# Second layer of a fused kernel: low parts of its weights on VectorE, conversion issued by steps, other banks and four buffers for its output blocks

## The chip, the cores and the metric

The kernel runs on one core of one Trainium2 chip. The time is that of the device for one run, in microseconds (us); shorter is better. A run is compared by the median of its executions. One further execution is profiled, and every row below comes from that one.

## What is computed

A gated linear attention over 4 batches of 8 heads, 768 positions and 48 features, then two feed-forward layers on 3072 tokens of 384 features, the first gated with 1536, the second with 2048 hidden features. All of it is in float32.

```python
def _attn_ref(q, k, v, f_logit):
    f = 1.0 / (1.0 + np.exp(-f_logit))
    for t in range(S):
        state = f[:, :, t, :, None] * state + np.einsum('bhd,bhe->bhde', k[:, :, t], v[:, :, t])
        y[:, :, t] = np.einsum('bhd,bhde->bhe', q[:, :, t], state)

def _moe_ref(x, w_gate, w_val, w_out):
    gate = 1.0 / (1.0 + np.exp(-(x @ w_gate)))
    return (gate * (x @ w_val)) @ w_out

def _moe2_ref(x, w_in, w_out):
    h = x @ w_in
    return (h * (1.0 / (1.0 + np.exp(-1.702 * h)))) @ w_out
```

## The kernel before, in words

**Products of two parts.** Each float32 product is made of three matmuls of a narrower type: every operand is a high part and a low part (the number less its high part), and `mm3` adds high x high, high x low and low x high in PSUM (lines 369 to 371, and 470 to 472 in the second layer's output). ScalarE makes the high parts, VectorE the low ones (`split`, lines 381 and 382). For each chunk of 128 hidden features of the second layer (`m2_in`), ScalarE applies the sigmoid (line 455), VectorE multiplies (line 456), then ScalarE and VectorE split the product into `gh` and `gl`. In the first layer `m1_gate` and `m1_val` do the same with two projections (lines 395 and 401).

**Weights.** They lie in memory as 64-bit numbers, in units of 3 x 384 columns; units 0 to 11 are the first layer's, 12 to 22 the second's. A unit is loaded by SyncE into a buffer `wd` (`w_load`; in the second layer there are two such buffers), turned into 32-bit numbers on VectorE by three instructions through one scratch tile `wt` (`w_conv`, lines 337, 341 and 344), and split (`w_split`): ScalarE writes the high part (line 351), and the low part is made by VectorE for units 0 to 11 and by GpSimd for units 12 to 22 (line 353). The split tile takes the place of a first-layer unit that TensorE has done with. Later every unit is loaded again for a check of its range (`w_check`, on ScalarE).

**Tiles and stages.** The first layer goes over the tokens in 8 tiles of 256 to 512, and attention runs beside it, some way ahead. The second layer goes over 6 tiles of 512 tokens in 16 chunks each; a chunk is a projection (9 matmuls of 512 columns) and, two chunks later, 12 matmuls of 384 columns into four output blocks (`m2_out`). The units 12 to 22 are converted while the last tile of the first layer runs, and a little beyond.

**PSUM.** Three banks in a ring hold projections (`ps_g`, tag `gv`). Three hold the first layer's output (`ps_x`, tags `x20`, `x21`, `x22`), which is copied out by ScalarE, VectorE and ScalarE in this order (lines 426 and 428); two are attention's (`ps_a`, tag `at`). In the second layer blocks 0 to 2 of a tile use `ps_x` and block 3 `ps_a`. Copies of the finished blocks (lines 476 and 478) go to three buffers `o`, and from there to memory by SyncE.

**Order.** Every step is put down with a position in a plan by `at(pos, ...)`, the steps are sorted by position and each engine gets its instructions in that order. `group(n)` is what the plan counts for 9 matmuls of n columns, `P8` the position of the last tile of the first layer, `P2` that of the second layer, `PACE2` the distance of two of the units 12 to 22. Steps of these units are held in that order on VectorE and ScalarE (`held_back`).

Of the kernel before, what the change touches and what calls it, by code (L numbers as in the profile page):

```python
# [48 lines left out]
PACE2 = 6.9  # L49
# [6 lines left out]
def fused_kernel(ctx, tc, qk, lf, vu, vn, wts, consts, out):  # L56
# [277 lines left out]
    def w_conv(u):  # L334

        lw, hw = st["wd", u][:, :, 0], st["wd", u][:, :, 1]
        nc.vector.tensor_scalar(
            out=wt, in0=hw, scalar1=3, scalar2=0x3FFFFFF8,
            op0=ALU.logical_shift_left, op1=ALU.bitwise_and,
        )  # L340
        nc.vector.scalar_tensor_tensor(  # L341
            out=wt, in0=hw, scalar=-0x40000000, in1=wt, op0=ALU.bitwise_and, op1=ALU.bitwise_or
        )
        nc.vector.scalar_tensor_tensor(  # L344
            out=lw, in0=lw, scalar=29, in1=wt, op0=ALU.logical_shift_right, op1=ALU.bitwise_or
        )

    def w_split(u):
        s = st.pop(("wd", u)).bitcast(F32)[:, :, 0]
        w = wp.tile([128, 2, WU], F32R, tag="w", name="w")  # L350
        nc.scalar.activation(out=w[:, 0], in_=s, func=AF.Copy)
        eng = nc.vector if u < NF1 else nc.gpsimd
        eng.tensor_tensor(out=w[:, 1], in0=s, in1=w[:, 0].bitcast(F32), op=ALU.subtract)  # L353
        for m in range(3):
            st["w", 3 * u + m] = w[:, :, DM * m:DM * m + DM]
# [103 lines left out]
    def m2_out(j, fc):  # L459
        gh, gl = st.pop(("g", L2 + j, fc))  # L460
        w = st["w", W2 + 2 * fc + 1]
        if fc == 0:
            st["ops"] = [
                (ps_x if k < 3 else ps_a).tile([128, DM], F32, tag=f"x2{k}" if k < 3 else "at", name="ops")
                for k in range(TT // 128)
            ]
        for m in range(TT // 128):
# [5 lines left out]
            if fc == NF2 - 1:  # L473
                o = st["late"].tile([128, DM], F32, tag="o", bufs=3, name="o")
                if m % 2 == 1:
                    nc.vector.tensor_copy(out=o, in_=ps)
                else:
                    nc.scalar.activation(out=o, in_=ps, func=AF.Copy)
                r0 = j * TT + m * 128
                nc.sync.dma_start(out=out[r0:r0 + 128, :], in_=o)  # L480
# [24 lines left out]
    def count():  # L505
        low, one = st["low"]
        cnt = ps_a.tile([1, 1], F32, tag="at", name="cnt")
# [140 lines left out]
    for u in range(NF1):  # L648
        p = need[u]
        at(p - 13, w_load, u)  # L650
        at(p - 7, w_conv, u)
        at(p - 5, w_split, u)
    for u in range(NF1, NU):
        p = P8 + 8 + (u - NF1) * PACE2
        at(p - 4, w_load, u)
        at(p, w_conv, u)
        at(p + 2, w_split, u)
# [6 lines left out]
    def held_back(pos, fn, args):  # L664
# [3 lines left out]
        if fn in (w_conv, w_split) and args[0] >= NF1:  # L668
# [297 lines left out]
```

## Time and profile before

| what | value |
| --- | --- |
| median of 3 runs | 1012.57 us (1011.74 to 1015.92) |
| the profiled execution, its own time | 1011.5 us |
| its span | 1009.7 us |
| mean granted clock of TensorE | 0.976 |
| TensorE busy | 966.4 us (96%) |
| VectorE busy | 621.8 us (62%) |
| ScalarE busy | 393.2 us (39%) |
| GpSimd busy | 150.1 us (15%) |

The span runs from the first to the last instruction; what is between it and the run's time lies outside of the trace. In rows, PE is TensorE, DVE VectorE, ACT ScalarE, POOL GpSimd and SP SyncE. Matmuls overlap one another, and the ends of them are modelled, so their pace is read from start to start. The clock is a share of full speed.

### The profile page before, as it was taken

What the parts mean: (1) busy time and instruction counts of PE and PEld (TensorE: products, weight loads), DVE (VectorE), ACT (ScalarE), POOL (GpSimd) and SP (SyncE); (2) the same over time, 40 slices, a digit from 0 to 9 for tenths busy, and PEclk for the clock granted to TensorE, in tenths of its full rate; (3) what the DMA queues carried; (4) which work ended last, traced back from release to release, by engine and by line L of the source; (5) the groups of instructions that cost most, each with busy time, mean ns of one, the idle gap of its engine ahead of it and who ended that gap; (6) DMA issues with size and microseconds to landing.
All of it is one profiled execution on the core that took longest, in us unless ns stands there. A gap on an engine that the chain in (4) does not pass through costs nothing.

```text
span 1009.7 us, 17235 instructions
## 1 busy us (share of the span) xinstructions
PE 966.4 (96%) x6978; PEld 857.7 (85%) x6978; DVE 621.8 (62%) x1073; ACT 393.2 (39%) x744; POOL 150.1 (15%) x157
## 2 busy tenths in 40 slices
PE   6689899999999999999999889999999999999997
PEld 4579899899999888888888668989999989999996
DVE  7799978876778767777658786343433433433332
ACT  3335333333343422232332326888632322322322
POOL 2311212312132312222104331000000000000000
PEclk8589999999999999999999999999999999999999
DMA  5664312221231321121033347787210000000001
GB/s 151 231 208 186 103 39 86 83 62 54 63 91 54 92 60 46 46 77 54 7 156 141 141 172 291 276 300 265 102 63 1 24 10 1 32 1 1 32 1 35
DMA packets 29736, 96.86 MB, mean 96 GB/s; under 512 B 4496, under 2 KB 16912, under 8 KB 23760
## 3 DMA queue, kind: packets, MB, share of 16 engines
q1 hardware_dynamic: 29504, 95.57, 28.3%
q8 instruction: 57, 0.93, 0.4%
q14 instruction: 31, 0.25, 0.1%
q10 hardware_dynamic: 144, 0.10, 0.0%
HBM read 84.25 MB, written 9.44 MB: 93 GB/s over the span
## 4 chain that ended last, share of the span: by engine, by line
PE 70%; DVE 13%; ACT 6%; DMA 5%; issue 5%; POOL 1%; SPq 0%; ACTq 0%; DVEq 0%; POOLq 0%
PE gv L369 13%; PE gv L371 12%; PE gv L370 12%; PE ops L470 6%; PE ops L472 6%; PE ops L471 5%; DMA wd<-in_wts 4%; PE x2ps L369 3%; PE x2ps L371 3%; PE x2ps L370 3%; PE yt L282 2%; PE sc L197 2%; DVE wt L341 2%; DVE wd L344 2%; DVE gl L382 1%
## 5 line engine op out<-in xcount | busy, mean ns | idle before, releaser
L369 PE MATMUL gv<-xh,w 128*128 128x512 f32 (+2 forms) x864 | 313.5, 363 | 7.6 <-DVE g L401 3.8
L371 PE MATMUL gv<-xh,w 128*128 128x512 f32 (+2 forms) x864 | 308.1, 358 | 1.0 <-DVE w L353 0.9
L370 PE MATMUL gv<-xl,w 128*128 128x512 f32 (+2 forms) x864 | 308.4, 357 | 0.6 <-DVE xl L314 0.4
L382 DVE TENSOR_TENSOR gl<-g,gh 128x512 fp32r<-128x512 f32 (+2 forms) x192 | 138.5, 723 | 117.8 <-ACT gh L381 91.5
L381 ACT ACTIVATE gh<-g 128x512 fp32r<-128x512 f32 (+2 forms) x192 | 110.5, 577 | 237.7 <-DVE g L401 173.0
L369 PEld LDWEIGHTS gv<-xh,w 128*128 128x128 f32 x864 | 164.3, 190 | 30.2 <-DVE g L401 4.6
L371 PEld LDWEIGHTS gv<-xh,w 128*128 128x128 f32 x864 | 163.4, 190 | 22.2 <-DVE w L353 1.6
L370 PEld LDWEIGHTS gv<-xl,w 128*128 128x128 f32 x864 | 164.4, 190 | 18.1 <-DVE xl L314 1.3
L456 DVE TENSOR_TENSOR g<-g,gv 128x512 f32<-128x512 f32 x96 | 66.0, 688 | 161.4 <-ACT g L455 161.4
L470 PE MATMUL ops<-w,gh 128*128 128x384 f32 x384 | 129.9, 338 | 1.3 <-ACT x L428 1.2
L472 PE MATMUL ops<-w,gl 128*128 128x384 f32 x384 | 129.6, 338 | 0.0
L471 PE MATMUL ops<-w,gh 128*128 128x384 f32 x384 | 129.0, 336 | 0.0
L455 ACT ACTIVATE g<-gv 128x512 f32<-128x512 f32 x96 | 57.0, 594 | 140.9 <-PE gv L371 140.9
L370 PE MATMUL x2ps<-gl,w 128*128 128x256 f32 (+2 forms) x288 | 97.6, 340 | 3.8 <-DVE gl L382 3.8
L369 PE MATMUL x2ps<-gh,w 128*128 128x256 f32 (+2 forms) x288 | 96.2, 339 | 1.4 <-ACT gh L381 1.4
L371 PE MATMUL x2ps<-gh,w 128*128 128x256 f32 (+2 forms) x288 | 96.8, 337 | 0.0
L395 ACT ACTIVATE g<-gv 128x256 f32<-128x256 f32 (+2 forms) x96 | 47.0, 489 | 122.4 <-PE gv L371 121.8
L232 DVE STREAM_TRANSPOSE kn<-kh 32x128 f32<-32x128 f32 x288 | 87.1, 302 | 4.2
L401 DVE TENSOR_TENSOR g<-g,gv 128x256 f32<-128x256 f32 (+2 forms) x96 | 52.6, 548 | 56.9 <-PE gv L371 55.1
L470 PEld LDWEIGHTS ops<-w,gh 128*128 128x128 f32 x384 | 72.1, 188 | 7.1 <-ACT x L428 1.6
L471 PEld LDWEIGHTS ops<-w,gh 128*128 128x128 f32 x384 | 72.1, 188 | 4.0
L472 PEld LDWEIGHTS ops<-w,gl 128*128 128x128 f32 x384 | 72.0, 188 | 0.3 <-DVE gl L382 0.3
(99 smaller groups left out, 1087.2 us busy)
## 6 DMA issues: line engine op xcount, KB each, us to landing
wd<-in_wts SPq DMA_DIRECT2D x46, 1152.0 KB, 5.2
QKF<-in_qk SPq DMA_DIRECT2D x42, 192.0 KB, 3.4
QKF<-in_lf SPq DMA_DIRECT2D x22, 256.0 KB, 2.9
vnt<-in_vn SPq DMA_DIRECT2D x24, 192.0 KB, 3.1
U<-in_vu SPq DMA_DIRECT2D x48, 96.0 KB, 2.7
x<-x2d SPq DMA_DIRECT2D x6, 768.0 KB, 5.6
out_y<-o SPq DMA_DIRECT2D x24, 192.0 KB, 1.9
x2d<-x SPq DMA_DIRECT2D x4, 768.0 KB, 3.8
```

The source lines that it names most:

```text
L232: nc.vector.transpose(out=kn[32 * b:32 * b + 32, :, 32 * a:32 * a + 32], in_=kh[32 * a:32 * a + 32, :, 32 * b:32 * b + 32],)
L369: nc.tensor.matmul(out=ps, lhsT=wh, rhs=xh, start=first, stop=False)
L370: nc.tensor.matmul(out=ps, lhsT=wh, rhs=xl, start=False, stop=False)
L371: nc.tensor.matmul(out=ps, lhsT=wl, rhs=xh, start=False, stop=last)
L381: nc.scalar.activation(out=gh, in_=g, func=AF.Copy)
L382: (eng or nc.vector).tensor_tensor(out=gl, in0=g, in1=gh.bitcast(F32), op=ALU.subtract)
L401: nc.vector.tensor_tensor(out=g, in0=g, in1=pv, op=ALU.mult)
L455: nc.scalar.activation(out=g, in_=ph, func=AF.Sigmoid, scale=1.702)
L456: nc.vector.tensor_tensor(out=g, in0=g, in1=ph, op=ALU.mult)
L470: nc.tensor.matmul(out=ps, lhsT=gh[:, ts], rhs=w[:, 0], start=fc == 0, stop=False)
L471: nc.tensor.matmul(out=ps, lhsT=gh[:, ts], rhs=w[:, 1], start=False, stop=False)
L472: nc.tensor.matmul(out=ps, lhsT=gl[:, ts], rhs=w[:, 0], start=False, stop=fc == NF2 - 1)
```

## The change

The low parts of units 12 to 22 move from GpSimd to VectorE. The three conversion instructions and the two of the split become steps of their own, at five positions instead of two, and the distance of two units grows from 6.9 to 7.4 of the plan. The blocks 0 and 1 of an output tile go to the two banks of `ps_a`, blocks 2 and 3 take turns through the three of `ps_x`; the one-value tile `cnt` moves to the ring of projections. There are four output buffers instead of three, and the copy of the very last block is made in two halves, by VectorE and ScalarE.

```diff
-PACE2 = 6.9
+PACE2 = 7.4
...
-    def w_conv(u):
+    def w_conv(u, step):
...
-    def w_split(u):
+    def w_high(u):
+        s = st["wd", u].bitcast(F32)[:, :, 0]
+        w = st["wu", u] = wp.tile([128, 2, WU], F32R, tag="w", name="w")
+        nc.scalar.activation(out=w[:, 0], in_=s, func=AF.Copy)
+
+    def w_low(u):
         s = st.pop(("wd", u)).bitcast(F32)[:, :, 0]
-        w = wp.tile([128, 2, WU], F32R, tag="w", name="w")
-        nc.scalar.activation(out=w[:, 0], in_=s, func=AF.Copy)
-        eng = nc.vector if u < NF1 else nc.gpsimd
-        eng.tensor_tensor(out=w[:, 1], in0=s, in1=w[:, 0].bitcast(F32), op=ALU.subtract)
+        w = st.pop(("wu", u))
+        nc.vector.tensor_tensor(out=w[:, 1], in0=s, in1=w[:, 0].bitcast(F32), op=ALU.subtract)
...
             st["ops"] = [
-                (ps_x if k < 3 else ps_a).tile([128, DM], F32, tag=f"x2{k}" if k < 3 else "at", name="ops")
-                for k in range(TT // 128)
+                (ps_a if m < 2 else ps_x).tile(
+                    [128, DM], F32, tag="at" if m < 2 else f"x2{(2 * j + m) % 3}", name="ops"
+                )
+                for m in range(TT // 128)
             ]
...
-                o = st["late"].tile([128, DM], F32, tag="o", bufs=3, name="o")
-                if m % 2 == 1:
+                o = st["late"].tile([128, DM], F32, tag="o", bufs=4, name="o")
+                if j == N2 - 1 and m == 3:
+                    nc.vector.tensor_copy(out=o[:, 0:192], in_=ps[:, 0:192])
+                    nc.scalar.activation(out=o[:, 192:], in_=ps[:, 192:], func=AF.Copy)
+                elif m % 2 == 1:
...
-        cnt = ps_a.tile([1, 1], F32, tag="at", name="cnt")
+        cnt = ps_g.tile([1, 1], F32, tag="gv", name="cnt")
...
     for u in range(NF1, NU):
         p = P8 + 8 + (u - NF1) * PACE2
         at(p - 4, w_load, u)
-        at(p, w_conv, u)
-        at(p + 2, w_split, u)
+        for step in range(3):
+            at(p + (0, 0.9, 2.4)[step], w_conv, u, step)
+        at(p + 3.8, w_high, u)
+        at(p + 5.2, w_low, u)
...
-        if fn in (w_conv, w_split) and args[0] >= NF1:
+        if fn in (w_conv, w_high, w_low) and args[0] >= NF1:
```

Nothing before unit 12 moves on any engine. The order of VectorE before, in the last tile of the first layer, from the product (`g`) of one chunk to the low half (`gl`) of the second after it (`wt` and `wd` are a unit's conversion):

```order
L401 TENSOR_TENSOR g<-g,gv 128x512
L382 TENSOR_TENSOR gl<-g,gh 128x512
L337 TENSOR_SCALAR wt<-wd 128x1152
L341 SCALAR_TENSOR_TENSOR wt<-wd,wt 128x1152
L344 SCALAR_TENSOR_TENSOR wd<-wd,wt 128x1152
L401 TENSOR_TENSOR g<-g,gv 128x512
L382 TENSOR_TENSOR gl<-g,gh 128x512
L337 TENSOR_SCALAR wt<-wd 128x1152
L341 SCALAR_TENSOR_TENSOR wt<-wd,wt 128x1152
L344 SCALAR_TENSOR_TENSOR wd<-wd,wt 128x1152
L401 TENSOR_TENSOR g<-g,gv 128x512
L382 TENSOR_TENSOR gl<-g,gh 128x512
```

The order of VectorE now, at the same place, three products with what stands between and behind them (`w` is a low part):

```order
L407 TENSOR_TENSOR g<-g,gv 128x512
L388 TENSOR_TENSOR gl<-g,gh 128x512
L347 SCALAR_TENSOR_TENSOR wd<-wd,wt 128x1152
L359 TENSOR_TENSOR w<-wd,w 128x1152
L407 TENSOR_TENSOR g<-g,gv 128x512
L388 TENSOR_TENSOR gl<-g,gh 128x512
L338 TENSOR_SCALAR wt<-wd 128x1152
L343 SCALAR_TENSOR_TENSOR wt<-wd,wt 128x1152
L347 SCALAR_TENSOR_TENSOR wd<-wd,wt 128x1152
L407 TENSOR_TENSOR g<-g,gv 128x512
L359 TENSOR_TENSOR w<-wd,w 128x1152
L388 TENSOR_TENSOR gl<-g,gh 128x512
```

Before, each product had a whole conversion behind it; now a conversion can lie on both sides of a product, and its low part follows on VectorE.

The order of VectorE now at the seam of the layers, from the copy of the first layer's middle block (`x`) on, two products of the second layer and what stands around them (`xl` are low parts of the second layer's next input):

```order
L432 COPY x_6425<-x2ps 128x512
L388 TENSOR_TENSOR gl<-g,gh 128x512
L338 TENSOR_SCALAR wt<-wd 128x1152
L343 SCALAR_TENSOR_TENSOR wt<-wd,wt 128x1152
L462 TENSOR_TENSOR g<-g,gv 128x512
L347 SCALAR_TENSOR_TENSOR wd<-wd,wt 128x1152
L388 TENSOR_TENSOR gl<-g,gh 128x512
L452 TENSOR_TENSOR xl<-x_6452,xh 128x512 x2
L359 TENSOR_TENSOR w<-wd,w 128x1152
L462 TENSOR_TENSOR g<-g,gv 128x512
L452 TENSOR_TENSOR xl<-x_6452,xh 128x512
L338 TENSOR_SCALAR wt<-wd 128x1152
```

Before, the same stretch had no low parts `w`, and its last unit came with the first of these chunks; now a unit more is converted here.

The last copies with their waits, ScalarE now (the names with numbers are buffers and blocks of the last tile; `o_9440` is the last):

```order
L489 ACTIVATE o_9422<-ops_9014 128x384 [waits DMAHW1_49,PE_49]
L489 ACTIVATE o_9434<-ops_9016 128x384 [waits DMAHW3_49,PE_49]
L485 ACTIVATE o_9440<-ops_9017 128x192 [waits DMAHW4_49,DMAHW0_49,DVE_49]
```

and VectorE now:

```order
L487 COPY o_9428<-ops_9015 128x384 [waits DMAHW2_49,PE_49]
L484 COPY o_9440<-ops_9017 128x192 [waits DMAHW4_49,PE_49]
```

VectorE's half waits for TensorE and for a buffer, ScalarE's half waits for VectorE. Before, VectorE copied the whole block.

## Rows read from the trace of the kernel before

**Rows 1.** Windows: stretch, then us, PE, PEld, DVE, ACT, POOL busy, PEclk, DMA.

```profile
565.00:570.00 5.00, 3.02 (x14) 2.19 (x13) 4.16 (x5) 0.85 (x2) 0.04 (x1) 1.00 0.64 236
595.00:600.00 5.00, 1.78 (x6) 1.25 (x7) 4.04 (x3) 1.38 (x3) 2.67 (x1) 0.96 0.18 31
600.00:605.00 5.00, 4.44 (x14) 3.19 (x12) 3.38 (x4) 2.17 (x4) 0.32 (x1) 0.70 0.87 362
```

**Rows 2.** Waits of PE, 540 to 660 us: total, times, longest.

```profile
PE gv L369 <- DVE g L401: 3.8, 2, 2.0
PE x2ps L370 <- DVE gl L382: 2.6, 2, 2.3
```

**Rows 3.** Windows, of the whole loss and of a stretch without waits.

```profile
558.29:608.18 49.89, 41.13 (x168) 31.50 (x166) 40.06 (x35) 17.48 (x26) 16.21 (x6) 0.97 0.43 161
575.67:587.91 12.24, 12.24 (x55) 10.13 (x54) 9.51 (x9) 4.18 (x6) 3.30 (x2) 1.00 0.45 177
```

**Rows 4.** Groups by line, DVE, 540 to 600 us: busy us, mean ns, idle before.

```profile
L341 DVE SCALAR_TENSOR_TENSOR wt<-wd,wt 128x1152 int32<-128x1152 int32 x8 | 15.7, 1958 | 0.3
L382 DVE TENSOR_TENSOR gl<-g,gh 128x512 fp32r<-128x512 f32 x8 | 12.5, 1566 | 7.2 <-ACT gh L381 7.2
L337 DVE TENSOR_SCALAR wt<-wd 128x1152 int32<-128x1152 int32 x8 | 9.8, 1224 | 2.8 <-DMA wd<-in_wts 2.8
...
L401 DVE TENSOR_TENSOR g<-g,gv 128x512 f32<-128x512 f32 x8 | 5.5, 682 | 0.9 <-ACT g L395 0.9
```

**Rows 5.** Groups by line, POOL, 540 to 600 us.

```profile
L353 POOL TENSOR_TENSOR w<-wd,w 128x1152 fp32r<-128x1152 f32 x7 | 19.6, 2794 | 38.6 <-ACT w L351 33.4 <-DMA wd<-in_wts 5.2
```

**Rows 6.** Timeline, DVE: start us, us, instruction, idle before.

```profile
569.81 0.69 DVE L382 TENSOR_TENSOR gl<-g,gh 128x512 fp32r<-128x512 f32 x1 [0.70 <-ACT gh L381]
...
595.92 2.75 DVE L382 TENSOR_TENSOR gl<-g,gh 128x512 fp32r<-128x512 f32 x1 [1.22 <-ACT gh L381]
```

**Rows 7.** Instructions on tile wd: min/median/max ns, first and last start us.

```profile
L337 DVE TENSOR_SCALAR wt<-wd x23: 742/751/3271, 36.5 to 607.8; 128x1152 int32<-128x1152 int32 x23
L341 DVE SCALAR_TENSOR_TENSOR wt<-wd,wt x23: 1343/1359/3760, 37.4 to 608.6; 128x1152 int32<-128x1152 int32 x23
L344 DVE SCALAR_TENSOR_TENSOR wd<-wd,wt x23: 1341/1359/3748, 39.2 to 610.5; 128x1152 int32<-128x1152 int32 x23
L351 ACT ACTIVATE w<-wd x23: 1228/1257/1301, 41.9 to 611.9; 128x1152 fp32r<-128x1152 f32 x23
...
L353 DVE TENSOR_TENSOR w<-wd,w x12: 1331/1356/1683, 43.2 to 130.1; 128x1152 fp32r<-128x1152 f32 x12
```

**Rows 8.** Timeline, POOL, the low part beside the second row of rows 6.

```profile
595.45 2.67 POOL L353 TENSOR_TENSOR w<-wd,w 128x1152 fp32r<-128x1152 f32 x1 [5.42 <-ACT w L351]
```

**Rows 9.** DMA issues of the page: KB each, median us to landing.

```profile
wd<-in_wts SPq DMA_DIRECT2D x46, 1152.0 KB, 5.2
```

**Rows 10.** Timeline, PE, the last projection's matmul and the first output block's.

```profile
604.05 0.39 PE L371 MATMUL gv<-xh,w 128*128 128x512 f32 x1
605.63 0.44 PE L470 MATMUL ops<-w,gh 128*128 128x384 f32 x1 [1.19 <-ACT x L428]
```

**Rows 11.** Windows, a stretch of the second layer.

```profile
750.00:800.00 50.00, 50.00 (x253) 45.28 (x252) 18.29 (x27) 15.97 (x28) 0.00 (x0) 1.00 0.00 1
```

**Rows 12.** Timeline of the end: the last matmul and the last copy.

```profile
1002.77 0.34 PE L472 MATMUL ops<-w,gl 128*128 128x384 f32 x1
1004.11 0.56 DVE L476 COPY o<-ops 128x384 f32<-128x384 f32 x1 [1.45 <-DMA out_y<-o]
```

**Rows 13.** Groups by line and shape, DVE, a copy of 256 columns.

```profile
L426 DVE COPY x<-x2ps 128x256 f32<-128x256 f32 x1 | 0.4, 409 | 0.0
```

**Rows 14.** Groups by line and shape, ACT, copies out of PSUM.

```profile
L298 ACT ACTIVATE xr<-yt 32x128 f32<-32x128 f32 x24 | 6.5, 269 | 0.3
...
L478 ACT ACTIVATE o<-ops 128x384 f32<-128x384 f32 x12 | 5.8, 479 | 3.2 <-PE ops L472 3.2
L428 ACT ACTIVATE x<-x2ps 128x512 f32<-128x512 f32 x8 | 4.7, 593 | 5.4 <-PE x2ps L371 5.4
```

More of the change, by code (lines that the diff above doesn't have):

```diff
@@ L332, in w_load @@
         st["wd", u] = d
-    def w_conv(u):
+    def w_conv(u, step):
         lw, hw = st["wd", u][:, :, 0], st["wd", u][:, :, 1]
[L337 to L346, printed above, removed]
-    def w_split(u):
+        if step == 0:
+            nc.vector.tensor_scalar(
+                out=wt, in0=hw, scalar1=3, scalar2=0x3FFFFFF8,
+                op0=ALU.logical_shift_left, op1=ALU.bitwise_and,
+            )
+        elif step == 1:
+            nc.vector.scalar_tensor_tensor(
+                out=wt, in0=hw, scalar=-0x40000000, in1=wt, op0=ALU.bitwise_and, op1=ALU.bitwise_or
+            )
+        else:
+            nc.vector.scalar_tensor_tensor(
+                out=lw, in0=lw, scalar=29, in1=wt, op0=ALU.logical_shift_right, op1=ALU.bitwise_or
+            )
+    def w_high(u):
[3 more added lines that the diff above has]
+    def w_low(u):
         s = st.pop(("wd", u)).bitcast(F32)[:, :, 0]
-        w = wp.tile([128, 2, WU], F32R, tag="w", name="w")
-        nc.scalar.activation(out=w[:, 0], in_=s, func=AF.Copy)
-        eng = nc.vector if u < NF1 else nc.gpsimd
-        eng.tensor_tensor(out=w[:, 1], in0=s, in1=w[:, 0].bitcast(F32), op=ALU.subtract)
+        w = st.pop(("wu", u))
+        nc.vector.tensor_tensor(out=w[:, 1], in0=s, in1=w[:, 0].bitcast(F32), op=ALU.subtract)
         for m in range(3):
@@ L463, in m2_out @@
             st["ops"] = [
-                (ps_x if k < 3 else ps_a).tile([128, DM], F32, tag=f"x2{k}" if k < 3 else "at", name="ops")
-                for k in range(TT // 128)
+                (ps_a if m < 2 else ps_x).tile(
+                    [128, DM], F32, tag="at" if m < 2 else f"x2{(2 * j + m) % 3}", name="ops"
+                )
+                for m in range(TT // 128)
             ]
@@ L650, in fused_kernel @@
         at(p - 13, w_load, u)
-        at(p - 7, w_conv, u)
-        at(p - 5, w_split, u)
+        for step in range(3):
+            at(p - 7, w_conv, u, step)
+        at(p - 5, w_high, u)
+        at(p - 5, w_low, u)
     for u in range(NF1, NU):
@@ L655, in fused_kernel @@
         at(p - 4, w_load, u)
-        at(p, w_conv, u)
-        at(p + 2, w_split, u)
+        for step in range(3):
+            at(p + (0, 0.9, 2.4)[step], w_conv, u, step)
+        at(p + 3.8, w_high, u)
+        at(p + 5.2, w_low, u)
     for u in range(NU):
```

## The prediction

> **What bounds the kernel now.** TensorE is busy 96% of the span, so time can only be won where it stands still. I read the views from coarse to fine: the busy table of the page, then 5-us windows over the seam between the two layers, then the waits of TensorE, then single rows. In [rows 1] the reader sees three windows in which TensorE works 3.02, 1.78 and 4.44 of 5 us, the last two at a granted clock of 0.96 and 0.70. [rows 2] names what it waited for there: VectorE's products `g` (3.8 us in two waits) and VectorE's low halves `gl` (2.6 us).
>
> The whole loss of this seam can be counted. Between 575.67 and 587.91 nothing waits: 54 matmuls of 512 columns in 12.24 us, 0.2267 us each [rows 3]. Between 558.29 and 608.18 the order holds 154 of these and 12 of 384 columns (168 with the ones at the edges). A step of the second layer, 9 of the one and 12 of the other, takes 4.15 us (253 matmuls in 50.00 us, 21 to a step, [rows 11]), which leaves 0.176 us for one of 384 columns. So 154 x 0.2267 + 12 x 0.176 = 37.0 us of work stand in 49.9 us: **12.9 us lost**. This is more than the named waits, since it holds short restarts and the fallen clock: the means of 0.96 and 0.70 [rows 1] make 0.4 and 3.0 us at 1.2 instead of 2.4 GHz, half of which, 1.7 us, is lost.
>
> Why VectorE is late there: it converts the second layer's weights, in units of 1152 columns. In [rows 4] its three long forms average 1958, 1566 and 1224 ns between 540 and 600 us, while the same instructions undisturbed take 1359 [rows 7], 690 [rows 6] and 751 ns [rows 7]. Eight of each: 8 x (0.60 + 0.88 + 0.47) = 15.6 us of stretch. GpSimd made 7 low parts in that time [rows 5], so each of them costs VectorE 2.2 us. One pair shows how: GpSimd's low part begins at 595.45 and ends at 598.12 [rows 8]; VectorE's `gl` begins at 595.92, takes 2.75 us instead of 0.69 and ends 0.55 us after GpSimd does [rows 6].
>
> In the old order most of these steps carry one whole unit between two products. That is 0.75 + 1.36 + 1.36 [rows 7], plus 2.2 of stretch, plus `gl` 0.69 and the product 0.68 [rows 4, 6]: 7.0 us, against 27 matmuls x 0.2267 = 6.12 us for TensorE. VectorE is the bound of this seam and falls back 0.9 us a step until TensorE waits.
>
> **The change part by part.**
>
> *Low parts on VectorE.* GpSimd's 11 instructions leave, 11 of 1.36 us come to VectorE (12 of that form ran on VectorE in the first layer, [rows 7]). They take the stretch of 2.2 us a unit with them, since GpSimd then has nothing left to do. VectorE's work for a unit goes from 3.47 + 2.2 = 5.7 to 3.47 + 1.36 = 4.83 us.
>
> *Pace and steps.* Units come every 7.4 instead of 6.9 of the plan's microseconds. The plan counts 0.4245 ns a column, 27 x 512 x 0.4245 ns = 5.87 us a step, and the trace shows 6.12, so a unit comes every 1.26 steps, 7.7 us. VectorE then needs 4.83 + 1.26 x (0.68 + 0.69) = 6.6 us of every 7.7, or 85%. The fullest steps of the new order (low part, `gl` and three conversion rows between two products) need 1.36 + 0.69 + 3.47 + 0.68 = 6.2 us against 6.12, and no more than two of them follow each other; the others need 4.1 to 4.8. None falls back as now. So the waits on `g`, `gl` and `gh` go, and the clock has no reason to fall. I take all of the 12.9 us as the gain, and look for what is late next.
>
> *What waits behind the new instructions.* A low part on VectorE waits for ScalarE's high part (1.26 us, [rows 7]) and holds the next product behind it. In most places `gl` or a product stands between, so 1.26 - 0.69 = 0.6 us of VectorE's time stays idle per unit: 85% becomes 93%. On SyncE a load of raw weights waits for the low part that frees its buffer. From a unit's first step to its low part's end it takes some 6.8 us, the load 5.2 us to land [rows 9] and 0.4 to issue, and the buffer's next turn comes after two units, 15.4 us: 3 us are left. The other loads on that queue (tiles of the second layer's input) are wanted tens of microseconds later. Cost nothing, covered by this gap. Units end about 5 us later by the plan; the last is wanted in the 15th step of the second layer, some 40 us after it is ready.
>
> *Output blocks.* Blocks 0 and 1 go to banks that attention has long left, so the old wait of 1.19 us for the first copy out of layer one [rows 10] has no place. Block 2 now takes the bank that the *last* copy empties, on ScalarE behind a `gh`. Its first matmul starts 16 slots after layer one's last one starts (10 x 0.2267 + 6 x 0.176 = 3.3 us). That last matmul ends 0.39 after its start and a copy takes 0.59 [rows 14], so the copy could end at 1.0 if the product before `gh` is on time, which leaves 2.3 us. One conversion row of 1.36 us ahead of the product fits, two don't. Bounds: 0 and 1.35 us (what that place loses today: 1.19 idle, and the 0.16 by which a matmul's modelled end, at 0.39, stands behind its slot, [rows 10]). In the five steps there (4.15 us each) VectorE's rows, split parts and the copy of `x` taken at 0.69 like `gl`, need 4.1, 4.2, 5.4, 4.2 and 4.1 us, 22.0 against 20.8: nearly full but with two steps of lag to spend. I take 0.5 us, nearer to zero, since the fallback is spread over the lag.
>
> The one-value count moved to the ring of three banks for projections takes a turn there once, whose next user comes three projections later. Nothing.
>
> *End.* The last output copy waits for a buffer: TensorE is done at 1002.77 + 0.34 = 1003.11, the copy begins at 1004.11 and takes 0.56 [rows 12], so it ends at 1004.67. With four buffers it can start at about 1003.15. Of the halves, VectorE's 192 columns lie below the 409 ns of 256 [rows 13]; the slope to 0.56 for 384 [rows 12] gives 0.34. ScalarE's lie between 269 ns for 128 and 479 for 384 [rows 14]: 0.32. Side by side they end at 1003.5, a gain of 1.2 us. But the new order shows a wait on VectorE at ScalarE's half: one after the other they end at about 1003.85. I take **0.8 us**, and keep 1.2 as the other end. At the ends of the other tiles the fourth buffer gives TensorE nothing, since it waits for no output copy there.
>
> No run here shows two engines reading one bank together. The Trainium skill, PSUM — Partial Sum Buffer, "PSUM bank collisions raise a hardware error", says that two engines on the same bank and quadrant at once are an error, reads against reads included; by it halves of one block must go one after the other, which is what the order shows, and the gain is 0.8.
>
> Sum against the profiled execution, 1011.5 us (span 1009.7): 12.9 - 0.5 + 0.8 = 13.2 us, so **998.3**. The median of the runs, 1012.57, stands 1.1 above that execution; I put about two thirds of it on the forecast: **999.0 us**.
>
> **The rivals.**
>
> *VectorE is full at the seam (20%).* For: 22.0 us of rows in 20.8 us, waits on ScalarE not counted. Against: before that stretch it has 7 to 15% to spare. Price: block 2 waits 1.35 us instead of 0.5, the 1.2 us of fallback become waits, and a clock that falls once costs 1.7 us as it does now. That is 3.8 more: about 1003.
>
> *The stretch is VectorE's own (7%).* If GpSimd didn't cause it, a unit costs 5.7 + 1.36, with products 8.8 us every 7.7. Over ten units 11 us are lost instead of 12.9; with the end's 0.8 this gives about 1009, no change. Against: the undisturbed rows of the same forms, and that the long ones end just after GpSimd's.
>
> The Trainium skill, Perfetto Trace Analysis, "Optimizing Scalar/DVE Operations", advises work off VectorE, even to GPSIMD, when VectorE is saturated, and adds that the two share a read port, so that it might not help. Taken by its first half the move is wrong and this rival or the next follows; the trace agrees with the second half, 2.2 us of stretch against 1.36 us of work.
>
> *Slower: VectorE stands before the low part (5%).* Same stretch, and each low part waits out ScalarE's high part of 1.26 us with the product queued behind: 10.1 us a unit every 7.7, 23 us lost over ten units instead of 12.9, about 1021. It decides from 9.0 us a unit on (7.7 + 1.3, where today's loss is reached); without the stretch even a full wait of 1.26 gives 7.9.
>
> That the change doesn't do what it says is left out: the order has GpSimd's 11 rows gone and VectorE's 11 there, and the last half's wait is counted.
>
> **How the numbers follow.** Forecast 68%, rivals 20, 7 and 5%. The range reaches from 996.5 (no wait at block 2, halves side by side, all of the median's offset left out) to 1005 (the first rival with the median's offset and a microsecond of waits in the first steps of the second layer). About 0.5% (5 us) is what a measurement of this kernel can tell from no change. Faster by more than that: the forecast and the first rival, 88%; within it 7%; slower 5%.
>
> **What would show it.** Right: between 558 and 608 us TensorE is busy in every window at a clock of 1.00; VectorE's long forms average 1.36, 0.69 and 0.75 us; GpSimd has no row after attention's last; the first output block waits for nothing; the last copy starts 0.05 us behind the last matmul and ScalarE's half behind VectorE's. Wrong: forms that stay stretched without GpSimd; a wait of `ops` on a copy of `x` of over 1.4 us; idle time of VectorE before its low parts of more than a microsecond each; a projection that waits for weights.

## The result, and the profile after

The changed kernel takes 997.5 us (median of four runs, 996.43 to 1000.45), the kernel before 1012.15 in the same comparison. The ratio is 0.9854 with a 95% interval of 0.982 to 0.9888: faster by 1.1 to 1.8%. One of the four executions of experiment 6 below took 1883.38 us; why is not known, and its median is that of the other three.

The profiled execution of the changed kernel took 1000.45 us, the longest of its four, with a span of 998.7. It need not be compared by its end: the first 450 us of the kernel vary by up to 4 us from run to run, while from 500 us on two executions of the changed kernel agree within hundredths (experiment 11). So I use a yardstick that every trace here has: from ScalarE's gate sigmoid in the first layer near 500 us (the 83rd of its kind) to the last one of the kernel (the 192nd). The timeline of ScalarE, before and after, each row with its start, its length and the idle time ahead of it:

```profile
500.34 0.60 ACT L395 ACTIVATE g<-gv 128x512 f32<-128x512 f32 x1 [2.72 <-PE gv L371]
...
996.94 0.60 ACT L455 ACTIVATE g<-gv 128x512 f32<-128x512 f32 x1 [2.20 <-PE gv L371]
```

```profile
503.00 0.60 ACT L401 ACTIVATE g<-gv 128x512 f32<-128x512 f32 x1 [2.71 <-PE gv L377]
...
985.74 0.60 ACT L461 ACTIVATE g<-gv 128x512 f32<-128x512 f32 x1 [2.20 <-PE gv L377]
```

It is 496.60 us before and 482.74 after: **13.86 us** gone. The seam alone, by windows over the same 168 matmuls as the first row of [rows 3], and the three windows of [rows 1], after the change (us, then PE, PEld, DVE, ACT, POOL busy, PEclk, DMA):

```profile
560.89:597.91 37.02, 37.02 (x168) 31.01 (x167) 31.24 (x34) 15.33 (x23) 0.00 (x0) 1.00 0.47 167
565.00:570.00 5.00, 5.00 (x24) 4.14 (x23) 3.73 (x5) 2.22 (x3) 0.00 (x0) 1.00 0.37 155
595.00:600.00 5.00, 5.00 (x27) 4.45 (x26) 4.96 (x7) 3.59 (x7) 0.00 (x0) 1.00 0.81 283
600.00:605.00 5.00, 5.00 (x27) 4.61 (x26) 5.00 (x8) 2.39 (x4) 0.00 (x0) 1.00 0.92 341
```

49.89 us have become 37.02, TensorE is never idle and its granted clock stays at 1.00. The list of TensorE's waits has no row from 500 us to the end, where [rows 2] stood. VectorE's groups from 540 to 600 us, against [rows 4]:

```profile
L343 DVE SCALAR_TENSOR_TENSOR wt<-wd,wt 128x1152 int32<-128x1152 int32 x8 | 10.9, 1357 | 0.2
...
L359 DVE TENSOR_TENSOR w<-wd,w 128x1152 fp32r<-128x1152 f32 x7 | 9.5, 1357 | 5.2 <-ACT w L354 5.2
L388 DVE TENSOR_TENSOR gl<-g,gh 128x512 fp32r<-128x512 f32 x11 | 7.6, 688 | 4.1 <-ACT gh L387 4.0
L338 DVE TENSOR_SCALAR wt<-wd 128x1152 int32<-128x1152 int32 x8 | 6.0, 753 | 0.0
```

The three long forms are back at 1357, 688 and 753 ns (from 1958, 1566 and 1224), and the low parts stand there with 1357 ns. The end of the kernel, all engines; to be read against [rows 12]:

```profile
991.57 0.34 PE L480 MATMUL ops<-w,gl 128*128 128x384 f32 x1
991.95 0.36 DVE L484 COPY o<-ops 128x192 f32<-128x192 f32 x1 [0.49 <-PE ops L480]
992.34 0.33 ACT L485 ACTIVATE o<-ops 128x192 f32<-128x192 f32 x1 [0.42 <-DVE o L484]
```

From the last matmul's start to the last copy's end it is 1.10 us instead of 1.90. But to the end of the span it is 998.7 - 991.57 = 7.13 us, and before it was 1009.7 - 1002.77 = 6.93.

### The profile page after: what moved, and what is told of

Same layout as the page of the kernel before. It is cut to its first block, busy times and chain, and to the rows that moved or that the text cites. A ratio compares the mean times of both kernels' runs of the same rounds, so it can differ in the third digit from the quotient of the medians.

```text
span 998.7 us, 17213 instructions
## 1 busy us (share of the span) xinstructions
PE 962.4 (96%) x6978; PEld 859.2 (86%) x6978; DVE 612.8 (61%) x1084; ACT 395.7 (40%) x745; POOL 116.6 (12%) x146
## 4 chain that ended last, share of the span: by engine, by line
PE 87%; DVE 7%; issue 2%; ACT 2%; DMA 1%; SPq 0%; ACTq 0%; DVEq 0%
PE gv L375 16%; PE gv L377 16%; PE gv L376 15%; PE ops L478 7%; PE ops L480 7%; PE ops L479 7%; PE x2ps L375 4%; PE x2ps L376 4%; PE x2ps L377 4%; PE yt L282 3%; PE sc L197 2%; PE dl L246 1%; DVE wd L347 1%; DMA xr<-ys 1%; DVE kn L232 1%
## 5 line engine op out<-in xcount | busy, mean ns | idle before, releaser
L388 DVE TENSOR_TENSOR gl<-g,gh 128x512 fp32r<-128x512 f32 (+2 forms) x192 | 129.5, 676 | 102.6 <-ACT gh L387 77.0
```

The costliest lines, as they stand in the source:

```text
L388: (eng or nc.vector).tensor_tensor(out=gl, in0=g, in1=gh.bitcast(F32), op=ALU.subtract)
```

## The experiments

Theory: GpSimd's low part holds VectorE up, that makes VectorE late, and TensorE's 12.9 us follow from it. First rival: the new steps and the slower pace won the time, and the engine of the low part is a side matter. Second rival: GpSimd's part cost time in another way than through VectorE. Experiments 3 and 12 are edits of the kernel before, 11 is the changed kernel as it is, and the others are edits of the changed kernel. All are read by the yardstick. Experiments 5 and 7 to 10 are single runs. The last column goes by a span given to 0.1 us, so it holds to 0.05 us:

| kernel | median or single run, us | yardstick, us | against after | last output matmul's start to end of span, us |
|---|---|---|---|---|
| before | 1012.15 | 496.60 | +13.86 | 6.93 |
| after | 997.5 | 482.74 | 0 | 7.13 |
| 1: low parts on GpSimd again | 1007.97 | 492.72 | +9.98 | 7.11 |
| 2: old places and pace | 998.12 | 482.74 | 0.00 | 6.99 |
| 3: before, engine alone changed | 998.71 | 482.74 | 0.00 | 7.29 |
| 4: added GpSimd subtraction | 1010.79 | 496.33 | +13.59 | 7.13 |
| 5: added GpSimd copy | 1003.81 | 489.11 | +6.37 | 6.86 |
| 6: added VectorE work | 1002.72 | 487.85 | +5.11 | 7.15 |
| 7: old banks | 996.20 | 482.75 | +0.01 | 6.93 |
| 8: three output buffers | 998.92 | 482.75 | +0.01 | 7.44 |
| 9: last copy whole, ScalarE | 997.07 | 482.74 | 0.00 | 6.68 |
| 10: matmuls behind the last | 998.69 | 482.74 | 0.00 | 7.06 |
| 11: after, once more | 997.84 | 482.74 | 0.00 | 7.13 |
| 12: before, three words changed | 998.27 | 483.25 | +0.51 | 6.92 |

**1. Low parts on GpSimd again.**

```diff
-        nc.vector.tensor_tensor(out=w[:, 1], in0=s, in1=w[:, 0].bitcast(F32), op=ALU.subtract)
+        (nc.vector if u < NF1 else nc.gpsimd).tensor_tensor(out=w[:, 1], in0=s, in1=w[:, 0].bitcast(F32), op=ALU.subtract)
```

> The changed kernel with one thing undone: the second layer's low parts of weights run on GpSimd again, with the new steps, pace, banks and buffers kept. Theory (GpSimd's low part stretches VectorE's long forms by 2.2 us a unit, and VectorE's load per unit decides the seam): the three long forms average 1.9 to 2.0, 1.5 to 1.6 and 1.2 us again between 540 and 600 us; VectorE needs 3.47 + 2.2 for a unit and 1.26 x 1.37 for products, 7.4 us of every 7.7, so it is nearly full and the unevenness of the steps shows: 2 to 8 us of waits come back, 1002 us (999 to 1006). Rival A (steps and pace won the time, the engine of the low part did not): 997 to 998.5 us, TensorE without waits at the seam, whatever the forms take. Rival B (the engine won all of it, steps and pace nothing): all of the 12.9 us come back, 1010 us.

Measured 1007.97 us (ratio to before 0.9966, 0.9952 to 0.998): 9.98 of the 13.86 us are back. Rival A falls, rival B is near, and my 1002 was too low. The forms averaged 1698, 1554 and 925 ns, where I had written 1.9 to 2.0, 1.5 to 1.6 and 1.2 us: the middle one alone came out. TensorE's waits from 500 us on, then two rows of ScalarE:

```profile
PE gv L375 <- ACT g L401: 1.9, 2, 1.5
PE ops L478 <- ACT x L434: 1.8, 1, 1.8
PE ops L478 <- ACT o L489: 1.7, 1, 1.7
PE ops L478 <- ACT gh L387: 0.6, 2, 0.4
```

```profile
580.47 1.26 ACT L354 ACTIVATE w<-wd 128x1152 fp32r<-128x1152 f32 x1 [2.03 <-DVE wd L347]
581.61 0.60 ACT L401 ACTIVATE g<-gv 128x512 f32<-128x512 f32 x1
```

VectorE is no longer the one that is waited for; ScalarE is. At 580.47 its high part has waited 2.03 us for VectorE's late conversion, and the sigmoid that TensorE wants (1.5 us of wait) stands behind it in the queue. The sum of VectorE's work, 7.4 us of every 7.7, said "nearly full"; in truth it was busy for 42.67 of 55 us here (545 to 600) while TensorE lost 3.5 of them:

```profile
545.00:600.00 55.00, 51.50 (x224) 41.28 (x222) 42.67 (x38) 19.16 (x27) 17.87 (x7) 1.00 0.40 146
```

**2. Old places and old pace, low parts on VectorE.**

```diff
-PACE2 = 7.4
+PACE2 = 6.9
...
-            at(p + (0, 0.9, 2.4)[step], w_conv, u, step)
-        at(p + 3.8, w_high, u)
-        at(p + 5.2, w_low, u)
+            at(p, w_conv, u, step)
+        at(p + 2, w_high, u)
+        at(p + 2, w_low, u)
```

> The changed kernel with the other thing undone: the conversion's three instructions of a unit at one place, high and low part at the next, and a unit every 6.9 of the plan's microseconds as before; the low parts stay on VectorE. Theory: no stretch (long forms 1.36, 0.69 and 0.75 us), VectorE needs 4.83 + 1.175 x 1.37 = 6.4 us of every 7.2, and 0.6 to 1.3 us more where the low part stands behind ScalarE's high part with little between: 7.0 to 7.7, close to full, 0 to 5 us of waits, 1000 us (997 to 1003). Rival A (steps and pace won the time): most of the 12.9 us come back, 1008 us or more. Rival B (the engine won all of it): 997 to 998.5 us.

Measured 998.12 us (0.9865, 0.9846 to 0.9884), and not one hundredth on the yardstick. Rival B holds: with the low parts on VectorE, places and pace change nothing. The low parts wait for ScalarE somewhat less than after the change, 5.8 us for nine against 5.2 for seven:

```profile
L359 DVE TENSOR_TENSOR w<-wd,w 128x1152 fp32r<-128x1152 f32 x9 | 12.2, 1358 | 5.9 <-ACT w L354 5.8
```

**3. The kernel before with the engine alone changed.**

```diff
-        eng = nc.vector if u < NF1 else nc.gpsimd
+        eng = nc.vector
```

> The kernel before with one word changed: the second layer's low parts of weights run on VectorE, and steps, pace, banks, buffers and the last copy stay as they were. Theory (the engine of the low part made the whole seam loss, and the other edits only lie beside it): TensorE waits for nothing between 550 and 610 us, from 500 us on the kernel runs as the changed one does but for 0 to 0.9 us in the first steps of the second layer (the small losses there that the kernel before shows); 997 to 999 us. Rival (steps, pace or banks carry part of the gain when all are old together): 999.5 us or more, with waits on x, g or gl at the seam.

Measured 998.71 us (0.9873, 0.9855 to 0.9891), the yardstick is that of the changed kernel. ScalarE's rows:

```profile
501.44 0.60 ACT L395 ACTIVATE g<-gv 128x512 f32<-128x512 f32 x1 [2.72 <-PE gv L371]
...
984.18 0.60 ACT L455 ACTIVATE g<-gv 128x512 f32<-128x512 f32 x1 [2.20 <-PE gv L371]
```

One line of the diff is the whole gain of 13.86 us, the small losses in the first steps of the second layer included. Steps, pace, banks and buffers are worth 13.86 - 9.98 = 3.9 us only while GpSimd does the low parts (before against experiment 1).

**4 and 5. GpSimd work that nobody waits for.**

```diff
+        if u >= NF1:
+            pr = st["late"].tile([128, WU], F32, tag="pr", bufs=1, name="pr")
+            h = w[:, 0].bitcast(F32)
+            nc.gpsimd.tensor_tensor(out=pr, in0=h, in1=h, op=ALU.subtract)
```

> The changed kernel, and behind each high part of the second layer's weights an added GpSimd subtraction of the same shape (128x1152, reads the high part twice, writes a tile that nobody reads). No instruction of another engine waits for it. Theory (GpSimd's access alone stretches VectorE): the added instruction takes some 2.7 us, VectorE's long forms grow by 2.2 us a unit to 1.9, 1.6 and 1.2 us in the mean or the low part of 1.36 us stretches in their place; VectorE then needs 4.83 + 2.2 + 1.73 = 8.8 us of every 7.7 and falls back 1.1 us a unit, 7 to 11 us of waits, 1007 us (1003 to 1010). Rival (the old order's dependence of VectorE and TensorE on GpSimd's result cost the time, or the long forms were long for another reason): 997 to 998.5 us and forms of 1.36, 0.69 and 0.75 us.

Measured 1010.79 us (0.999, 0.998 to 1.0): the gain is gone. No other engine reads `pr`, the order of instructions on VectorE, ScalarE and TensorE is that of the changed kernel, and ScalarE's keep their lengths (`gh` 629 ns in the mean, 630 after the change, from 503 to 640 us). Of the two engines' instructions only VectorE's are longer, so the second rival falls, and it is GpSimd's access alone. Groups of VectorE and GpSimd, 540 to 600 us (GpSimd to 610), and meetings from the timeline of both:

```profile
L392 DVE TENSOR_TENSOR gl<-g,gh 128x512 fp32r<-128x512 f32 x8 | 11.4, 1426 | 4.0 <-ACT gh L391 4.0
L338 DVE TENSOR_SCALAR wt<-wd 128x1152 int32<-128x1152 int32 x7 | 11.0, 1569 | 0.0
...
L362 POOL TENSOR_TENSOR pr<-w 128x1152 f32<-128x1152 f32 x8 | 24.6, 3076 | 48.6 <-ACT w L354 48.6
```

```profile
563.94 1.36 DVE L363 TENSOR_TENSOR w<-wd,w 128x1152 fp32r<-128x1152 f32 x1 [0.71 <-ACT w L354]
564.05 3.21 POOL L362 TENSOR_TENSOR pr<-w 128x1152 f32<-128x1152 f32 x1 [5.43 <-ACT w L354]
565.21 2.60 DVE L392 TENSOR_TENSOR gl<-g,gh 128x512 fp32r<-128x512 f32 x1
...
572.68 2.11 POOL L362 TENSOR_TENSOR pr<-w 128x1152 f32<-128x1152 f32 x1 [5.42 <-ACT w L354]
...
602.37 3.21 POOL L362 TENSOR_TENSOR pr<-w 128x1152 f32<-128x1152 f32 x1 [5.91 <-ACT w L354]
603.54 0.68 DVE L466 TENSOR_TENSOR g<-g,gv 128x512 f32<-128x512 f32 x1
604.91 1.22 DVE L392 TENSOR_TENSOR gl<-g,gh 128x512 fp32r<-128x512 f32 x1
```

The low part that began 0.11 us ahead of GpSimd ran at its usual 1.36, and GpSimd's row took 3.21 us, against 2.11 at 572.68 where no VectorE row was ahead of it. The next one on VectorE, `gl`, took 2.60 instead of 0.69 and ended 0.55 us after GpSimd's row. Who starts first keeps going; the other stands. That holds for VectorE instructions with all their tensors in SBUF. The product `g`, with one input in PSUM, began in the middle of GpSimd's row at 603.54 and took its usual 0.68; so did the copy of `x` out of PSUM at 604.13 (0.68), and `gl` behind them was long again. This is why `g` stands at 682 ns in [rows 4] beside three stretched forms. The Trainium skill says this of the pair of ports that VectorE and GpSimd share (SBUF — State Buffer, "SBUF: two separate sides"): whoever starts first has it for the whole instruction and the other blocks, where VectorE's instruction has two SBUF inputs or runs in a mode that uses both of its ports. The trace agrees: `gl`, with two such inputs, is held up (2.60 us), and `g`, with one, is not (0.68). That the one-input row `wt` is held up too (1569 ns) would need such a mode, which no run here shows by itself. How much the pair costs a kernel the Trainium skill doesn't say; here it is 13.59 us for 11 such instructions.

Experiment 5 puts a plain copy in the subtraction's place:

```diff
-            h = w[:, 0].bitcast(F32)
-            nc.gpsimd.tensor_tensor(out=pr, in0=h, in1=h, op=ALU.subtract)
+            nc.gpsimd.tensor_copy(out=pr, in_=w[:, 0].bitcast(F32))
```

> The changed kernel with GpSimd's added instruction a plain copy (128x1152, reads the high part once, writes a tile that nobody reads) instead of a subtraction with two inputs. If any SBUF access of GpSimd holds VectorE up: each copy stretches the VectorE form that begins during it, to near the copy's end, and 5 to 12 us come back, in proportion to the copy's length. If it takes an instruction with two inputs: forms of 1.36, 0.69 and 0.75 us, no waits of TensorE between 500 us and the end, 997 to 1000 us.

Measured 1003.81 us: 6.37 of the 13.86 us are back, as the first of the two said. VectorE's and GpSimd's groups, over the same stretches:

```profile
L391 DVE TENSOR_TENSOR gl<-g,gh 128x512 fp32r<-128x512 f32 x10 | 9.4, 937 | 4.1 <-ACT gh L390 4.0
L338 DVE TENSOR_SCALAR wt<-wd 128x1152 int32<-128x1152 int32 x7 | 7.2, 1023 | 0.0
...
L361 POOL COPY pr<-w 128x1152 f32<-128x1152 f32 x8 | 16.2, 2020 | 50.7 <-ACT w L354 50.7
```

The copy, 2.02 us instead of 3.08 (1.15 instead of 2.11 where no VectorE row was ahead of it), does it too, and less; TensorE's waits are 2.9 us for a copy of `x` and 0.7 for `gl`. Summed over the timeline, the eleven GpSimd rows lengthen VectorE's by 16.0 us in experiment 4 and by 7.2 here (rows over 0.3 us longer than their form undisturbed), and TensorE lost 13.59 and 6.37 us, 0.85 and 0.88 of the stretch.

**6. The same time as plain work on VectorE.**

```diff
+        st["raw"] = st["wd", u]
...
+        if u >= NF1:
+            hw = st["raw"][:, :, 1]
+            nc.vector.tensor_scalar(
+                out=wt, in0=hw, scalar1=3, scalar2=0x3FFFFFF8,
+                op0=ALU.logical_shift_left, op1=ALU.bitwise_and,
+            )
+            nc.vector.scalar_tensor_tensor(
+                out=wt, in0=hw, scalar=-0x40000000, in1=wt, op0=ALU.bitwise_and, op1=ALU.bitwise_or
+            )
         nc.vector.tensor_tensor(out=w[:, 1], in0=s, in1=w[:, 0].bitcast(F32), op=ALU.subtract)
```

> The changed kernel, and ahead of each low part of the second layer's weights VectorE does the first two conversion instructions of the same unit once more (0.75 + 1.36 = 2.1 us, into the scratch tile that nobody reads any more): as much time as GpSimd's stretch took, as plain work. Theory (it is VectorE's load per unit that decides, whatever fills it): 8.7 us of every 7.7, less the idle time before the low part that the added work fills (0.6 a unit), 5 to 10 us of waits on products and low halves, 1005 us (1001 to 1009), with forms of 1.36, 0.69 and 0.75 us; the time is near that of the run with GpSimd's added subtraction. Rival (GpSimd's low part hurt by something other than the time it took from VectorE): 997 to 999 us, no waits.

Measured 1002.72 us (0.9905, 0.9882 to 0.9927). VectorE works 54.38 of 55 us from 545 to 600 and TensorE misses nothing there; the second row is the same stretch of experiment 4:

```profile
545.00:600.00 55.00, 55.00 (x249) 46.19 (x248) 54.38 (x60) 22.62 (x31) 0.00 (x0) 1.00 0.43 159
...
545.00:600.00 55.00, 49.22 (x206) 39.19 (x205) 46.26 (x39) 14.85 (x22) 18.18 (x6) 0.97 0.39 137
```

The only wait comes later (3.0 us for a product); 5.11 us are lost in all, where 2.1 us a unit were added. The time is not near that of experiment 4, as I had written. Here a full VectorE was cheaper than a stretched one that was 16% idle (46.26 of 55 us in experiment 4). One caution: the order of VectorE's instructions is set when the kernel is built, and with the added work in sight it came out differently, while a stretch is in no plan. Whether the same work in unchanged order would cost what the stretch costs was not tried and stays open.

**7. Old banks.**

```diff
-                (ps_a if m < 2 else ps_x).tile(
-                    [128, DM], F32, tag="at" if m < 2 else f"x2{(2 * j + m) % 3}", name="ops"
-                )
-                for m in range(TT // 128)
+                (ps_x if k < 3 else ps_a).tile([128, DM], F32, tag=f"x2{k}" if k < 3 else "at", name="ops")
+                for k in range(TT // 128)
...
-        cnt = ps_g.tile([1, 1], F32, tag="gv", name="cnt")
+        cnt = ps_a.tile([1, 1], F32, tag="at", name="cnt")
```

> The changed kernel with the output blocks and the one-value count in their old banks. Theory (the old wait of 1.19 us for a copy out of layer one was itself late because ScalarE was): in the changed kernel the first of these copies ends near 593.2 us, 2.6 us before the first output block's first matmul at 595.8, so the old banks cost nothing, less than 0.05 us between 500 us and the last matmul. Rival A (the banks were worth their wait): 1.0 to 1.3 us lost at the first block. Rival B (the banks carry the small losses of 0.93 us in the first steps of the second layer that the kernel before has and the changed one has not): 0.5 to 0.9 us lost between the 1st and the 17th step.

0.01 us on the yardstick: the banks carry nothing. The wait of 1.19 us in [rows 10] came of ScalarE's lateness, which went with GpSimd: before, the copy waited for ended at 605.58, behind a `gh` that had waited 6.45 us for VectorE's `g`; after the change the same copy ends at 593.20, 2.6 us ahead of the block's first matmul. Experiment 3, on the old banks too, has no such wait.

**8 and 9. The end: three buffers, and the last copy whole.**

```diff
-                o = st["late"].tile([128, DM], F32, tag="o", bufs=4, name="o")
+                o = st["late"].tile([128, DM], F32, tag="o", bufs=3, name="o")
```

> The changed kernel with three output buffers again; the last copy stays halved. Prediction's step: the last copy waits for a buffer, so from the last matmul's start to the end of the last copy it takes 1.8 to 2.0 us instead of 1.1, and the span ends 0.8 us later. Theory now (the end's gain is given back, because the last output's packets then move while an instruction load of 16 KB is on a DMA queue, which begins 1.07 us after TensorE's end in both kernels): the last copy ends 0.8 us later, but from the last matmul's start to the end of the span it is 6.9 us, as in the kernel before (6.93), and not more than the changed kernel's 7.13.

```diff
-                    nc.vector.tensor_copy(out=o[:, 0:192], in_=ps[:, 0:192])
-                    nc.scalar.activation(out=o[:, 192:], in_=ps[:, 192:], func=AF.Copy)
+                    nc.scalar.activation(out=o, in_=ps, func=AF.Copy)
```

> The changed kernel with its last output copy whole, on ScalarE. From rows: the copy starts 0.38 us behind the last matmul's start and takes 0.49, so it ends at 0.87 instead of 1.10. If the end's gain reached the span, the span would end 0.23 us sooner after the last matmul. Theory (the last output's packets are held by the instruction load of 16 KB, which starts 2.0 to 2.5 us after the last matmul's start in every run): the copy ends 0.23 sooner, but a few of its packets still come in 4.2 to 4.6 us after the last matmul's start, and the span ends 6.85 to 7.2 us after it, no change.

With three buffers the wait is there again, and the copy ends 991.71 - 989.66 = 2.05 us after the last matmul's start:

```profile
990.99 0.36 DVE L484 COPY o<-ops 128x192 f32<-128x192 f32 x1 [1.44 <-DMA out_y<-o]
```

Of 0.95 us that the copy is later, 7.44 - 7.13 = 0.31 reach the end of the span; I had written none. The whole copy on ScalarE ends 0.24 sooner, and the span 0.45 sooner (6.68; 6.92 in experiment 12), where I had written no change. The runs with four buffers and halves lie between 6.86 and 7.15, those with the old end at 6.93 and 7.29, so differences of 0.3 us can't be told from scatter here. The landing of the last output says it better: counted from the last matmul's start it comes after 4.92 us before, 4.97 after, 4.92 in experiment 8 and 4.74 in experiment 9, though the copies end between 0.87 and 2.05 us. What holds an early copy back is to be seen in the DMA view, in three stretches of half a microsecond after the change, from 993.5, 994.5 and 995.0 us on (the row of queue 8 is one load of instructions), then the issue of the last output:

```profile
q8 instruction: 1, 0.02, 19.9%
...
DMA packets 0, 0.00 MB, mean 0 GB/s; under 512 B 0, under 2 KB 0, under 8 KB 0
...
q1 hardware_dynamic: 5, 0.01, 6.3%
...
out_y<-o SPq DMA_DIRECT2D x1, 192.0 KB, 3.9
```

A load of 16 KB of instructions runs from 993.66 to 995.25; between 994.5 and 995.0 nothing of the output moves, and its last nine packets come one by one from 995.23 up to 996.1. In all ten profiles with an early copy (all but before and experiments 3, 8 and 10) the nine packets resume within 0.02 us of the load's end. The last output lands 3.9 us after its issue, where it took 3.0 before:

```profile
out_y<-o SPq DMA_DIRECT2D x1, 192.0 KB, 3.0
```

The transfer lost 0.9 us, all that the copy had won. Such a load starts 2.0 to 2.5 us after the last matmul's start in every profile but that of experiment 10, whether the copy is early or late; my 1.07 us after TensorE's end doesn't come out, it is 1.7 or more from the end of the last matmul's row. The Trainium skill (Runtime: NRT & Kernel Launch, "Instruction fetch mechanics") says that instructions come in blocks of 16 KiB by DMA; that such a block holds up a kernel's own packets it doesn't say, the trace shows it.

**10. Matmuls behind the last one.**

```diff
+    idle = ps_g.tile([128, 512], F32, tag="gv", name="idle")
+    xh = st["xh", L2 + N2 - 1]
+    for _ in range(8):
+        nc.tensor.matmul(
+            out=idle, lhsT=st["w", NW - 1][:, 0, 0:128], rhs=xh[:, 0], start=True, stop=True
+        )
```

> The changed kernel with eight more matmuls of 512 columns (0.23 us each, 1.8 us; their result is read by nobody) behind the last one that writes the output. Theory (the instruction load follows TensorE's end, and the last output's packets wait behind it): the load of 16 KB starts 1.8 us later, 3.9 us after the last output matmul's start; the packets of the last output no longer wait and are all in after 3.0 to 3.3 us instead of 4.5, its landing takes 2.0 instead of 3.9 us. Rival (the packets are late for another reason, such as four outputs on the queues at once): they still come in after 4.4 to 4.6 us.

Half of this came out. The load did move with TensorE's end, to 3.9 us after the last output matmul's start, and the last output's packets no longer stop for it; its landing took 2.7 us:

```profile
out_y<-o SPq DMA_DIRECT2D x1, 192.0 KB, 2.7
```

But the issue itself came a microsecond late, 1.3 instead of 0.35 us after the last copy, so that the packets were in after 4.3 us, not 3.3. It stood in SyncE's queue behind the issue before it, which took 1.58 us instead of 0.37:

```profile
990.10 1.58 SPq L491 DMA_DIRECT2D out_y<-o  x1
```

The load ahead of the one in question had moved too, from 1.3 us before the last output matmul's start to 0.06 behind it, and ran until 1.58; the three outputs before the last landed 3.5 to 4.0 us after their issues instead of 1.9 to 2.0. So the added matmuls moved one load out of the way of the last output and another into the way of the outputs before it. The load holds output up where they meet; that the end of the span would come sooner without the meeting is not shown.

**11 and 12. The changed kernel once more, beside the simplest version.**

```diff
-        eng = nc.vector if u < NF1 else nc.gpsimd
+        eng = nc.vector
...
-                o = st["late"].tile([128, DM], F32, tag="o", bufs=3, name="o")
-                if m % 2 == 1:
+                o = st["late"].tile([128, DM], F32, tag="o", bufs=4, name="o")
+                if m % 2 == 1 and (j, m) != (N2 - 1, 3):
```

> The changed kernel once more, beside the simple version below. From the sigmoid of the gate near 500 us to the last one 482.74 us as in its first trace; the last matmul of the output starts 7.0 us (6.85 to 7.2) before the end of the span; 997 to 998 us.

> The kernel before with three words changed: the low parts on VectorE, four output buffers, the very last copy on ScalarE; no steps, no new pace, no new banks, no halved copy. Theory (the engine is all of the gain at the seam, and the end gives at most some tenths): 482.74 us from the sigmoid near 500 us to the last one, 6.7 to 7.1 us from the last matmul's start to the end of the span, 997 to 998 us, the same as the changed kernel within the interval. Rival (the other edits carry something the single run on the engine alone did not show): 999 us or more.

997.84 us (0.9869, 0.9852 to 0.9885) and 998.27 (0.9867, 0.985 to 0.9883): the same. The simple version loses 0.51 us where I expected nothing; its list of waits shows 0.2 of them, an output block that waits for ScalarE's copy out of its bank. Experiment 3 doesn't lose it; ScalarE's order came out differently in the two, and which of the edits makes the loss was not tried. No version here beats the changed kernel by more than the measurement can tell.

## Why the prediction was right, point by point

**The seam, 12.9 us.** Right in size and cause. The work in the stretch was taken as 37.0 us from undisturbed matmuls; it measured 37.02, a gain of 49.89 - 37.02 = 12.87. That GpSimd's low part is the cause is shown from both sides: taken away alone it gives everything (experiment 3), put back as work that nobody needs it takes 13.59 of the 13.86 us (experiment 4). That the two are so near may be chance, since in experiment 4 VectorE has its own low parts besides; the shorter copy of experiment 5 takes less, as it should.

**How VectorE loses the time.** The step was mis-sized. "7.0 us a step" left out the idle 1.22 us that stands in the second row of [rows 6], where `gl` waits for `gh`, which waits behind the high part on ScalarE. The `gl` one step ahead of that row:

```profile
587.80 2.78 DVE L382 TENSOR_TENSOR gl<-g,gh 128x512 fp32r<-128x512 f32 x1 [1.25 <-ACT gh L381]
```

The two begin 8.12 us apart, against 6.12 for TensorE: VectorE fell back 2.0 us, not 0.9. The forecast didn't suffer, since the loss had been counted on TensorE and not summed from VectorE. The expectation for experiment 1 did: it went by the same sum of busy times, and missed by 6 us. The price of 2.2 us a unit was also a little high: summed over the whole timeline, eleven GpSimd rows lengthened VectorE's by 21.1 us before and by 17.3 in experiment 1, 1.9 and 1.6 each. It depends on when the next VectorE instruction that works in SBUF alone comes up after GpSimd's start.

**Pace and steps.** The prediction reasoned that the fullest steps just fit (6.2 against 6.12 us), and so they did; idle time before the low parts was put at 0.6 us and measured 0.63 in the mean of eleven. "About 5 us later by the plan" counts the pace alone; with the later place of the low part the last unit ends some 8 us later there, and still nothing waited for it. What the prediction didn't say is that old steps and pace fit as well (experiment 2, 0.00 us).

**Output blocks, a wait of 0.5 us taken.** It was 0. VectorE had one row ahead of the product, the low part at 592.12, as "one fits, two don't" allows. The copy ended at 595.23, the block's first matmul came at 596.87 with no idle time:

```profile
592.12 1.36 DVE L359 TENSOR_TENSOR w<-wd,w 128x1152 fp32r<-128x1152 f32 x1 [0.72 <-ACT w L354]
...
594.65 0.58 ACT L434 ACTIVATE x<-x2ps 128x512 f32<-128x512 f32 x1
...
596.87 0.33 PE L478 MATMUL ops<-w,gh 128*128 128x384 f32 x1
```

That the new banks end the 1.19 us wait was right in effect and wrong in reason: the old banks would have done (experiment 7).

**The first steps of the second layer.** Not foreseen: 13.86 - 12.87 = 1.0 us more than the seam. Read from matmul to matmul, the kernel before lost 0.25 us there at 623.3 and 0.7 between 673.1 and 675.2, at the first output matmuls of the second tile; the list of waits doesn't name them. They went with the engine (experiment 3); by what way is open.

**The end, 0.8 us.** Right at the copy (1.90 to 1.10 us, one half after the other), wrong at the span: 6.93 became 7.13. The step that failed is the silent one, that what ends sooner also lands sooner. The last output took 3.9 us to land instead of 3.0, with an instruction load in its way. The 0.2 us at the span is itself within the scatter of that column.

**The sum.** 12.9 - 0.5 + 0.8 = 13.2 us predicted; 12.87 + 1.0 + 0 - 0.2 = 13.7 measured. The errors of +1.0, +0.5 and -1.0 nearly cancel, which is luck. The medians differ by 14.65 us; the rest is no more than the first 500 us vary by, and was not looked into. The forecast of 999.0 was 1.5 above the 997.5.

**The rivals.** VectorE was not too full: it was busy for 4.96 and 5.00 of 5 us from 595 to 605 us, and TensorE waited for nothing; where it was filled on purpose (experiment 6), it lost 5.1 us only with 2.1 us more a unit. The stretch was not VectorE's own: the forms are at 1357, 688 and 753 ns. It did not stand long before the low part: 5.2 us for seven.

## What to carry to other kernels

Before moving work to GpSimd to relieve VectorE, compare VectorE's forms with and without a GpSimd row beside them: here each row of 2.8 us on GpSimd saved VectorE 1.36 and cost it 1.9 in the mean and up to 2.5. Look at the instructions that work in SBUF alone; those that read PSUM kept their lengths here. Count a loss on the engine that bounds the kernel, against its own undisturbed stretch, and not from the busy time of the engine that is late: the idle time in a chain over two in-order queues belongs to the step as well. When one line of a many-part change may carry it all, run that line alone first.

## What the runs showed that I had not expected

GpSimd's plain copy, 2.02 us, holds VectorE up as well (`gl` 937 instead of 688 ns in the mean), not only its two-input instruction. A VectorE at 54.38 of 55 us let TensorE run without a gap, while one at 46.26 of 55 cost it 5.8 us in the same stretch. VectorE's instructions that read PSUM ran through GpSimd's rows at full pace, 0.68 us. And an instruction load of 16 KB kept a 192 KB output from landing for 0.9 us.
